# A shared ring for loads, checks and low halves, a sixth bonus by VectorE, and a new issue order

## The chip, the cores and the metric

One core of a Trainium2 chip runs the whole program. The metric is device time in microseconds (us) of one execution, lower is better; the number quoted for a kernel is the median of its runs.

## The reference

Two parts follow each other. The first is a recurrence over 768 steps for 4 batches and 8 heads of 48; the second is a gated MLP with a spatial product over the sequence.

```python
for t in range(S):
    kt, vt, rt, wt = (k[:, :, t], v[:, :, t], r[:, :, t], w[:, :, t])
    cur = np.einsum('bhd,bhe->bhde', u[None] * kt, vt)
    y[:, :, t] = np.einsum('bhd,bhde->bhe', rt, state + cur)
    state = wt[:, :, :, None] * state + np.einsum('bhd,bhe->bhde', kt, vt)
...
h = np.maximum(x @ w_in, 0.0)
u, v = (h[..., :d_ff // 2], h[..., d_ff // 2:])
...
v_n = (v - mu) / np.sqrt(var + 1e-06)
v_s = np.einsum('ts,bsd->btd', w_spatial, v_n) + b_spatial[None, :, None]
gated = u * v_s
return (gated @ w_out).astype(np.float32)
```

`x` is `y` with its heads laid side by side (384 columns), `d_ff` is 1024, all arrays are fp32. The part of `cur` with `u` adds, at each step and head, (sum over d of r·u·k) times v. It is called the bonus below.

## The kernel before, in words

**The recurrence in 24 slots.** The sequence is cut into chunks of 128 steps, so a batch has 6 and the program has 24 slots, i = 0 to 23. `slot_load` (L406 to L420) brings a slot's w (W, L415), k and r (kr, L416), in most slots r and k once more in natural order (N, 384 KB, L419), and v (L420). `slot_prep` (L433 to L537) prepares them: pairwise products of w (W2, L471), k and r scaled by w (L475), two scans F and E (L478, L483), the scaling of k and r by them (L485, L489). `slot_a` multiplies k by r within chunks of 64 on TensorE (PE, L552) and VectorE (DVE) puts the result under a mask into the matrix AS (L556); `slot_kt` transposes k (L571), `slot_y` and `slot_inter` multiply AS and the state by v and r (L588), and products L644 with L659, L670 and L672 carry the state on. `slot_x` collects `y` (L692, L699), transposes it (L704) and splits it into fp32r high and low halves `xT` (L715, L718, L723).

**The bonus, in two ways.** For i < B_PE = 6, `rk` = r·k (L443) goes through four fp32 products with u on PE (`pg`, L448), DVE multiplies v by the sums (`bv`, L518), and one fp32 product with the unit matrix adds `bv` to `y` in PSUM (L598). From slot 6 on the sums come from the natural order: N·N (L496), times u (L498), a sum over each head (L500), small copies (`dgs`, L524), which are put on the diagonal of AS (L532 on ScalarE, L534 on DVE or GpSimd); so the product with AS holds the bonus. At slot B_PE the part of PSUM that L598 began is cleared once (L602).

**The checks of w.** 16 loads Nw of 384 KB (L429) and one ScalarE instruction each (L430) see to it that w is in the range for which the fast way is right.

**The gMLP.** Products of three fp32r passes (`mm3`, L728 to L730: high·high, high·low, low·high): `ph` (v half of the hidden layer), `pu` (u half), `pv` (spatial product, on `vh` and `vl`, L804), `po` (output). `g_unit` adds the bias on DVE (L978), multiplies by u (L980), and splits into gh and gl (L983); `out_unit` copies `po` out (L997) and stores (L1006), the first SPLIT = 8 outputs in two halves of 64 rows. The last batch takes a different arrangement of the products, with s1, s4 and q2.

**What sets the order.** Every operation is recorded with the engines that could do it. The string PLAN holds one word for each: a letter for the engine and a rank in base 36. Operations are issued in the order of the rank, and each engine and each queue keeps that order: SP issues all loads and stores, one behind the other. ZEROS puts runs of zero products (L1084) at given points of PE's stream. They write to an unused part of PSUM.

**Buffers.** A `Buf` names a tag, and a tag a ring of so many places. When the order is known, `place` gives each buffer the place whose last reader comes first in the order. A load into a place then waits for that reader. N, Nw, `rk` and q2 have the tag "N" with one place; the low halves of `xT`, s1 and s4 and the raw loads of two of the weight groups share "xT1" with three places; gh and gl have five places each.

Of the kernel before, what the change touches and what calls it, by code (L numbers as in the profile page):

```python
# [9 lines left out]
F32R = mybir.dt.float32r  # L10
I32 = mybir.dt.int32
# [9 lines left out]
DM = H * D  # L21
# [85 lines left out]
"""  # L107

ZEROS = """
1:8 d:5 u:7 1a:7 1o:5 1y:6 2j:2 f8:1  # L110
"""

FILL_TO = 5

EARLY = 8

W3 = 5

KR, AB = 3, 2

SPLIT, PE_END = 8, 10

B_PE = 6

LOW_T, SUM_T = {}, 0

Q = 32
T = D - Q

class Buf:

# [107 lines left out]
def kernel(  # L241
# [15 lines left out]
    P = 128  # L257
# [148 lines left out]
    def slot_load(i):  # L406
# [4 lines left out]
        if i >= B_PE:  # L411
            N = q["N"] = buf(p2, [P, 2, DM], "N", f"N{i}", 1)
# [812 lines left out]
```

## Time and profile before

| | |
|---|---|
| time, median of 3 runs | 356.73 us (356.66 to 357.18) |
| profiled execution, its own time | 358.06 us |
| its span | 356.3 us |
| PE busy, products | 348.8 us (98%) |
| DVE busy | 282.0 us (79%) |
| ACT, POOL busy | 218.5 us (61%), 134.7 us (38%) |
| DMA | 50.17 MB, mean 141 GB/s |

PE is the matrix engine TensorE, PEld its weight loads, DVE is VectorE, ACT is ScalarE, POOL is GpSimd, SP issues the DMAs (SPq is its queue). Busy times are of one profiled execution; neighbouring products on PE overlap in the records, so the distance from start to start says what one costs in a row. A releaser, behind "<-", is what ended an engine's wait. L12 is line 12 of the kernel.

### The profile page before, as it was taken

The page shows a single profiled execution, that of the slowest core. Times are in us where ns is not written, and L with a number is a line of the kernel's source. Part 1 is how long each engine was busy: PE and PEld are TensorE (multiplying, and loading weights), DVE is VectorE, ACT ScalarE, POOL GpSimd, SP SyncE. Part 2 cuts the span into 40 slices and gives each one's busy share as a digit, 9 for nine tenths or more (in the row PEclk, how much of TensorE's full clock was granted, in tenths as well). Part 3 has the DMA queues.
Part 4 walks back from the last instruction along what each step waited for, and adds up shares of the span by engine and source line. Part 5 has one row for each costly group of instructions (what it writes and reads, how often), then busy time and mean ns, then how long its engine had stood idle before and what let it go on. Part 6 is the DMA issues. An engine that isn't in the chain of part 4 may idle for free.

```text
span 356.3 us, 11397 instructions
## 1 busy us (share of the span) xinstructions
PE 348.8 (98%) x4638; PEld 324.9 (91%) x4638; DVE 282.0 (79%) x634; ACT 218.5 (61%) x594; POOL 134.7 (38%) x188
## 2 busy tenths in 40 slices
PE   7999899999999999999999899999999999999998
PEld 7887798999999889899989799899998998899997
DVE  7999998989969798898965889467655679879771
ACT  5559977986556786886455764772427538574230
POOL 2364262115671632231172444335643810402540
PEclk9999999999999999999999999999999999999999
DMA  7867776634545667464464355264422344211013
GB/s 213 269 191 220 227 208 206 210 116 118 162 124 166 166 174 229 146 183 124 106 207 119 115 146 147 53 204 129 130 68 89 93 126 129 54 62 43 2 44 116
DMA packets 23736, 50.17 MB, mean 141 GB/s; under 512 B 3200, under 2 KB 12544, under 8 KB 23680
## 3 DMA queue, kind: packets, MB, share of 16 engines
q1 hardware_dynamic: 23536, 49.21, 46.8%
q8 instruction: 37, 0.61, 0.8%
q10 hardware_dynamic: 144, 0.20, 0.1%
q14 instruction: 19, 0.16, 0.1%
HBM read 44.67 MB, written 4.72 MB: 139 GB/s over the span
## 4 chain that ended last, share of the span: by engine, by line
PE 79%; DVE 7%; DMA 5%; issue 4%; ACT 2%; POOL 1%; SPq 0%; DVEq 0%; ACTq 0%; POOLq 0%
PE pv L730 6%; PE pv L728 6%; PE pv L729 6%; PE py L588 6%; PE po L728 4%; PE po L730 4%; PE po L729 4%; PE pu L728 4%; PE pu L730 4%; PE pu L729 4%; PE ph L728 4%; PE ph L730 4%; PE ph L729 4%; PE paw L552 3%; PE pt L571 2%
## 5 line engine op out<-in xcount | busy, mean ns | idle before, releaser
L728 PE MATMUL pv<-ws,vh 128*128 128x384 f32 x144 | 49.4, 343 | 0.0
L730 PE MATMUL pv<-ws,vl 128*128 128x384 f32 x144 | 48.9, 340 | 0.1
L729 PE MATMUL pv<-ws,vh 128*128 128x384 f32 x144 | 48.6, 338 | 0.0
L728 PE MATMUL po<-wo,gh 128*128 128x384 f32 x96 | 33.3, 346 | 1.4 <-DVE t L978 1.3
L728 PE MATMUL pu<-xT,wi 128*128 128x384 f32 x96 | 33.1, 345 | 0.0
L730 PE MATMUL pu<-xT,wi 128*128 128x384 f32 x96 | 32.4, 337 | 0.0
L729 PE MATMUL pu<-xT,wi 128*128 128x384 f32 x96 | 32.3, 336 | 0.0
L730 PE MATMUL po<-wo,gl 128*128 128x384 f32 x96 | 32.3, 336 | 0.0
L729 PE MATMUL po<-wo,gh 128*128 128x384 f32 x96 | 32.2, 336 | 0.0
L728 PE MATMUL ph<-wi,xT 128*128 128x512 f32 x72 | 29.2, 405 | 0.0
L730 PE MATMUL ph<-wi,xT 128*128 128x512 f32 x72 | 28.3, 393 | 0.0
L729 PE MATMUL ph<-wi,xT 128*128 128x512 f32 x72 | 28.2, 391 | 0.0
L730 PEld LDWEIGHTS pv<-ws,vl 128*128 128x128 f32 x144 | 27.0, 188 | 0.6 <-DVE vl L804 0.6
L728 PEld LDWEIGHTS pv<-ws,vh 128*128 128x128 f32 x144 | 27.1, 188 | 0.4 <-ACT vh L802 0.3
L729 PEld LDWEIGHTS pv<-ws,vh 128*128 128x128 f32 x144 | 27.1, 188 | 0.2
L475 POOL TENSOR_TENSOR kr<-kr,W 112x256 f32<-112x256 f32 x19 | 17.1, 904 | 25.3 <-DMA kr<-in_tr_dram 9.6
L758 ACT ACTIVATE hv<-ph 128x512 f32<-128x512 f32 x24 | 14.3, 596 | 16.7 <-PE ph L730 16.4
L532 ACT ACTIVATE AS<-id,dgs 128x64 f32<-128x64 f32 x68 | 18.1, 337 | 6.9 <-DVE dgs L524 5.6
L978 DVE TENSOR_TENSOR t<-pv,b_sb 128x384 f32<-128x384 f32 x24 | 13.2, 552 | 11.4 <-PE pv L730 10.2
L670 ACT ACTIVATE S<-S,prod 112x48 f32<-112x48 f32 x72 | 18.2, 323 | 5.7 <-DVE S L659 3.2
L728 PEld LDWEIGHTS po<-wo,gh 128*128 128x128 f32 x96 | 18.0, 188 | 2.7 <-DVE t L978 1.6
L430 ACT ACTIVATE Nw<-Nw,few 128x768 f32<-128x768 f32 x16 | 15.0, 938 | 7.8 <-DVE prod L480 2.5
(265 smaller groups left out, 1047.1 us busy)
## 6 DMA issues: line engine op xcount, KB each, us to landing
kr<-in_tr_dram SPq DMA_DIRECT2D x24, 448.0 KB, 4.9
N<-in_nat_dram SPq DMA_DIRECT2D x18, 384.0 KB, 3.3
Nw<-in_gt_dram SPq DMA_DIRECT2D x16, 384.0 KB, 3.4
W<-in_tr_dram SPq DMA_DIRECT2D x24, 225.8 KB, 4.0
v<-in_nat_dram SPq DMA_DIRECT2D x24, 192.0 KB, 3.9
out_dram<-ot SPq DMA_DIRECT2D x15, 192.0 KB, 2.0
wst<-in_w_spT_dram SPq DMA_DIRECT2D x12, 192.0 KB, 5.8
a<-in_w_spT_dram SPq DMA_DIRECT2D x12, 192.0 KB, 2.4
```

What stands on the lines that cost most here:

```text
L430: op({"A": 0.95}, lambda: nc.scalar.activation(flat(), flat(), AF.Relu, bias=neg, accum_out=over[:, n:n + 1]), r=[(w, 0)], w=[(w, 0), ("ov ...
L475: op({"G": 0.9, "V": dve(half)}, lambda e, n=n: e.tensor_tensor(two(kr()[:R, n])[:, :, :, n], two(kr()[:R, n])[:, :, :, n], w_()[:, :, :, ...
L532: e.mul(As()[:, j, g, :], id64, dgs()[:, j, g:g + 1])
L552: nc.tensor.matmul(pa()[ks, j, g * L:(g + 1) * L], kr()[rs, 0, ts_], kr()[rs, 1, ts_], start=True, stop=True)
L571: nc.tensor.transpose(pt()[:, g, :], kr()[:R, 0, g * C:(g + 1) * C], ident[:R, :R])
L588: nc.tensor.matmul(py()[row][L * a:L * (a + 1), D * n:D * (n + 1)], x, z, start=(a, row) not in started, stop=not left[0], skip_group_chec ...
L670: e.mul(S1[i % 2][a][:, g, :], S0[:, g, :], Wc[:, g:g + 1])
L728: nc.tensor.matmul(ps, ah, bh, start=first, stop=False, **skip)
L729: nc.tensor.matmul(ps, ah, bl, start=False, stop=False, **skip)
L730: nc.tensor.matmul(ps, al, bh, start=False, stop=last, **skip)
L758: op({"A": 0.61}, lambda: nc.scalar.activation(hv(), ph(), AF.Relu, accum_out=col(0)), r=[(ph, 0)], w=[(hv, 0), (s, 0, j)])
L978: op({"V": dve(HT)}, lambda: nc.vector.tensor_tensor(t1(), pv()[:, :HT], b_sb[:, tsl], ALU.add), r=[(pv, 0), ("b", 0)], w=[(t1, 0)])
```

## The change

The tag "N" goes. N, Nw, `rk` and q2 take places in the ring "xT1", which now has four. The ring of gl has four places instead of five. B_PE is 5: slot 5 takes the second way to the bonus, with a load of N more and no `rk`, `pg`, `bv`. SPLIT is 7: one output fewer is stored in two halves. PLAN and ZEROS are new; ZEROS holds 36 zero products for 41.

```diff
-1:8 d:5 u:7 1a:7 1o:5 1y:6 2j:2 f8:1
+b:9 h:4 n:2 12:8 1m:4 1y:6 3c:3
...
-SPLIT, PE_END = 8, 10
+SPLIT, PE_END = 7, 10
...
-B_PE = 6
+B_PE = 5
...
-        d = buf(pm, [P, KX * HT], raw, f"d_{key}", 3, I32)
+        d = buf(pm, [P, KX * HT], raw, f"d_{key}", 3 + (raw == "xT1"), I32)
...
-            N = q["N"] = buf(p2, [P, 2, DM], "N", f"N{i}", 1)
+            N = q["N"] = buf(pm, [P, 2, DM], "xT1", f"N{i}", 4)
...
-        w = buf(p2, [P, 2, DM], "N", f"Nw{n}", 1)
+        w = buf(pm, [P, 2, DM], "xT1", f"Nw{n}", 4)
...
-            rkt = buf(p2, [P, 2, DM], "N", f"rk{i}", 1)
+            rkt = buf(pm, [P, 2, DM], "xT1", f"rk{i}", 4)
...
-            xT[b, h] = tuple(buf(pm, [P, KX, HT], f"xT{q}", f"xT{b}_{h}_{q}", 3, F32R) for q in range(2))
+            xT[b, h] = tuple(buf(pm, [P, KX, HT], f"xT{q}", f"xT{b}_{h}_{q}", 3+q, F32R) for q in range(2))
...
-        q2 = buf(p2, [P, 2, DM], "N", "q2", 1)
+        q2 = buf(pm, [P, 2, DM], "xT1", "q2", 4)
...
-        gh, gl = gg[b, h, f] = tuple(buf(pm, [P, HT], n, f"{n}{b}_{h}_{f}", 5, F32R) for n in ("gh", "gl"))
+        gh, gl = gg[b, h, f] = tuple(buf(pm, [P, HT], n, f"{n}{b}_{h}_{f}", 5 - (n == "gl"), F32R) for n in ("gh", "gl"))
```

The new order moves operations on every engine. Three places follow, as names of tiles with their numbers (a slot's, or batch, half and part).

**PE, at the products of slot 5 with v.** Before, from the transposes of slot 4's `y`:

```order
L704 MATMUL yt4_1014<-ident_94,y4_949 128x128 x3
L718 MATMUL yt3_978<-xT0_1_0_1022,nident_110 128x384
L598 MATMUL py0_88<-bv5_974,ident_94 128x384
L718 MATMUL yt4_1014<-xT0_1_0_1022,nident_110 128x384
L588 MATMUL py0_88<-v5_875,AS1_86 64x48
L588 MATMUL py1_89<-v5_875,AS1_86 64x48
```

and now:

```order
L571 MATMUL pt6_1071<-ident_94,kr6_979 128x112 x4
L718 MATMUL yt4_1023<-xT0_1_0_859,nident_110 128x384
L588 MATMUL py0_88<-v5_967,AS1_86 64x48
L588 MATMUL py1_89<-v5_967,AS1_86 64x48
L588 MATMUL py1_89<-vs5_984,AS1_86 64x48
```

The product with `bv5` (L598) and, further ahead, the four of `pg5` are gone; the first product of slot 5 begins on the cleared PSUM.

**SP, the loads from N17 to v17.** Before:

```order
L419 DMA N17_3161<-in_nat_dram 128x768
L416 DMA kr17_3168<-in_tr_dram 112x1024
L420 DMA v16_3226<-in_nat_dram 128x384
L415 DMA W18_3320<-in_tr_dram 112x516
L429 DMA Nw9_3325<-in_gt_dram 128x768
L420 DMA v17_3330<-in_nat_dram 128x384
L419 DMA N18_3365<-in_nat_dram 128x768
```

and now:

```order
L420 DMA v16_3104<-in_nat_dram 128x384
L419 DMA N17_3106<-in_nat_dram 128x768
L416 DMA kr17_3129<-in_tr_dram 112x1024
L419 DMA N18_3205<-in_nat_dram 128x768
L429 DMA Nw10_3226<-in_gt_dram 128x768
L415 DMA W18_3301<-in_tr_dram 112x516
L420 DMA v17_3364<-in_nat_dram 128x384
```

N18 stood behind the check Nw9 and behind v17, and now stands right behind kr17, ahead of both.

**DVE, ahead of the sum for `y8`.** Before:

```order
L983 TENSOR_TENSOR gl0_1_0_1903<-t10_1_0_1549,gh0_1_0_1896 128x384
L475 TENSOR_TENSOR kr10_1893<-kr10_1893,W10_1801 112x256 x2
L482 RECIPROCAL zz_80<-prod_133 112x8
L659 TENSOR_TENSOR S0_116<-paw_87,S110_119 112x192
L997 COPY ot0_0_1_1999<-po0_0_1_1822 128x384
L483 SCALAR_TENSOR_TENSOR E10_2011<-W2p_83,zz_80 112x256
L715 CAST xT1_0_0_1797<-yt7_1995 128x3x128
L556 COPY_PREDICATED AS1_86<-mask_130,paw_87 128x512
L659 TENSOR_TENSOR S0_116<-paw_87,S111_120 112x192
L699 TENSOR_TENSOR y8_2014<-y8_2014,py1_89 128x384
```

and now:

```order
L997 COPY ot0_0_2_1981<-po0_0_2_1804 128x384
L983 TENSOR_TENSOR gl0_1_0_1984<-t10_1_0_1686,gh0_1_0_1915 128x384
L534 TENSOR_TENSOR AS0_85<-id64_107,dgs10_1789 128x256
L471 TENSOR_TENSOR W2p_83<-W11_1923 112x256
L556 COPY_PREDICATED AS1_86<-mask_130,paw_87 128x512
L534 TENSOR_TENSOR AS0_85<-id64_107,dgs10_1789 128x256
L659 TENSOR_TENSOR S0_116<-paw_87,S110_119 112x192
L692 COPY y8_2038<-py0_88 128x384
L496 TENSOR_TENSOR N12_1844<-N12_1844 128x384
L478 SCALAR_TENSOR_TENSOR F11_2041<-zz_80,W2p_83 112x256
L500 TENSOR_REDUCE dg11_2043<-N11_1770 128x8
L699 TENSOR_TENSOR y8_2038<-y8_2038,py1_89 128x384
```

Ahead of `y8` now also stand a third output copy, L471 and L478 for slot 11, N12's product and the sum `dg11`, and y8's first copy (L692), which ACT did before; the scan for `E10` and its reciprocal have gone further ahead, the copy into `xT1_0_0` to ScalarE. `gl0_1_0` has moved behind `ot0_0_2`.

## Rows read from the trace of the kernel before

**Rows 1.** The page: busy time, share and count of each engine; DVE's slices.

```profile
PE 348.8 (98%) x4638; PEld 324.9 (91%) x4638; DVE 282.0 (79%) x634; ACT 218.5 (61%) x594; POOL 134.7 (38%) x188
...
DVE  7999998989969798898965889467655679879771
```

**Rows 2.** Table by stages: stretch, length, busy us (count) of PE, PEld, DVE, ACT, POOL, clock, DMA.

```profile
0.00:72.00 72.00, 67.55 (x1114) 59.64 (x1115) 65.92 (x148) 53.05 (x139) 25.61 (x43) 1.00 0.73 216
72.00:125.00 53.00, 52.64 (x720) 49.76 (x719) 44.52 (x100) 36.00 (x110) 25.51 (x32) 1.00 0.51 144
...
195.00:207.00 12.00, 10.74 (x163) 10.10 (x162) 9.92 (x24) 8.58 (x25) 4.64 (x6) 1.00 0.42 121
```

**Rows 3.** Chain of waits, 188 to 205 us: start, us, what.

```profile
193.16 5.32 DMA N<-in_nat_dram
...
199.09 1.15 DVE dgs L524
...
202.38 0.47 DVE t L978
...
202.90 0.44 PE po L728
```

**Rows 4.** PE's waits (releaser, total us, times, longest); DVE's timeline at 198 us.

```profile
PE paw L552 <- issue: 1.3, 1, 1.3
PE po L728 <- DVE t L978: 1.3, 1, 1.3
...
198.50 0.56 DVE L496 TENSOR_TENSOR N<-N 128x384 f32<-128x384 f32 x1 [1.30 <-DMA N<-in_nat_dram]
```

**Rows 5.** SP's waits: whole span, then 185 to 203 us; the page's DMA issues of N.

```profile
SPq L419 <- ACT Nw L430: 23.9, 7, 5.1
...
SPq L420 <- PE py L588: 5.3, 1, 5.3
...
N<-in_nat_dram SPq DMA_DIRECT2D x18, 384.0 KB, 3.3
```

**Rows 6.** Timeline of PE at slot 5's bonus: start, us, instruction.

```profile
44.54 1.05 PE L448 MATMUL pg<-up_sb,rk 112*128 112x2 f32 x8
45.45 0.42 PE L728 MATMUL pu<-xT,wi 128*128 128x384 f32 x1
...
56.13 0.81 PE L598 MATMUL py<-bv,ident 128*128 128x384 f32 x2
56.68 0.44 PE L718 MATMUL yt<-xT,nident 128*128 128x384 f32 x1
```

**Rows 7.** Zero products in the chain of waits at 17 us.

```profile
17.19 1.31 PE py L1084 x10
```

**Rows 8.** DVE by form: line, shapes, xcount, busy us, mean ns, idle before.

```profile
L475 DVE TENSOR_TENSOR kr<-kr,W 112x256 f32<-112x256 f32 x29 | 13.5, 469 | 0.0
L489 DVE TENSOR_TENSOR kr<-kr,E 112x512 f32<-112x512 f32 x16 | 11.4, 710 | 0.2
...
L496 DVE TENSOR_TENSOR N<-N 128x384 f32<-128x384 f32 x14 | 8.0, 573 | 1.5 <-DMA N<-in_nat_dram 1.5
...
L498 DVE TENSOR_TENSOR N<-N,u_sb 128x384 f32<-128x384 f32 x13 | 7.2, 551 | 0.1
...
L518 DVE TENSOR_TENSOR bv<-v,pg 128x384 f32<-128x384 f32 x6 | 3.3, 542 | 0.0
...
L443 DVE TENSOR_TENSOR rk<-kr 112x512 f32<-112x512 f32 x4 | 2.8, 690 | 0.2 <-DMA kr<-in_tr_dram 0.2
```

**Rows 9.** POOL's N·u by form; POOL and DVE side by side (timelines).

```profile
L498 POOL TENSOR_TENSOR N<-N,u_sb 128x384 f32<-128x384 f32 x5 | 5.4, 1089 | 13.7 <-DVE N L496 13.2 <-ACT y L692 0.5
...
123.95 1.06 POOL L485 TENSOR_TENSOR kr<-kr,F 112x496 f32<-112x496 f32 x1
...
124.59 0.83 DVE L496 TENSOR_TENSOR N<-N 128x384 f32<-128x384 f32 x1
...
198.82 1.40 POOL L804 TENSOR_TENSOR vl<-hv,vh 128x512 fp32r<-128x512 f32 x1 [1.56 <-ACT vh L802]
```

More of the change, by code (lines that the diff above doesn't have):

```diff
@@ new lines @@
+Aaa Aab S54 S4z S5y S7v V6k V6j V67 V6y V75 V78 V7h V72 G7o G6i V6p V6s A8r A81 V80 A7c A7q G8l A8n T87 V8w G8j T7i
+A7n V8z T9b T7w V8v V99 T9g A9j V9k T9m A9s Ta3 Aa6 Taf Tag Tak Aar Aas Aat Aau Vb8 Vbd Vbf Vbg Gbk Vbn Vbs Abx Aby
+Vc5 Ac1 Acb Vcc Ack Acp Vcr Tnz T5m T63 T65 A66 Tc6 Tcd Tcf Tcu Td7 Td8 Vdu Ved Aem Vey T69 T6h T6l A71 Tc7 Tcn Tco
+Tcz Td0 Tdd Vdo Gfw Ag8 Vg9 T6x T70 T7j A8b Tdc Tdl Tdm Tdn Tdt Tdz Veq Ves Agd Vgm T7r T7s T8d A8u Tc2 Tce Tcw Tcx
+Td4 Td5 Vd6 Vdr Af2 Ggb Tgu Tgw Tgy Tgz Vh6 Shx Thj Thl Thm Ti0 Vi3 Skc Thc The Ti2 Tim Vj3 Slo Tac Taq Tb5 Aba Tfa
@@ new lines @@
+V118 G11h V121 V172 G15x V13m A127 A14x A13n G14y T15a V15y G166 T124 V125 T173 T159 V167 G16a V16c T174 A17g V17h
+T17r A17s V17t T183 T184 T18a A191 A192 A194 A19c V19l V19t V1a5 V1a6 G1aa G1ae G1af A1am V1b0 A1b4 V1br V1ag V1av
+A1cq G1d0 A1ba V1bg A1ci V1d9 S18p A1a2 S12q S154 S10e S15t G142 V158 V16s V143 V144 V15h V15n G15i G16x G136 G137
+V147 V16o A165 V148 V150 A16e G18k G16i T16y V18o A16r T15j V15p T190 T16z V178 G17b V186 T195 A1ak V1ao T1b1 V1be
+V1bf T1c1 T1c2 T1c4 A1cr A1cs A1df S14q A14r S13o S170 S12j S189 G162 G17u V176 V16g V177 V18j V18n G185 V1a8 G12t
@@ L107 @@
+T1gv T1h6 V1hb T1gk T1h3 T1h4 V1ha T1gq T1gy T1h0 V1hs V1i1 A1i8 V1i9 T1gt T1hc T1hf V1hh V1hx A1i6 G1ih T1hk T1hl
+T1hm V1ho V1ir A1is V1iz T1hg T1hr T1hv V1i2 V1iw A1j1 V1j2 T1ht T1hw T1i3 V1id G1ie A1if G1il T1i4 T1i5 T1i7 V1ij
+G1im A1in V1iv T1i0 T1ia T1ib T1ii A1ik S1ji T1hn T1ic T1ip T1iq V1j3 S1j5 T1he T1ig T1io T1it A1iu S1j4 T1jd T1je
+T1jf T1jk A1jl S1jo T1ix T1iy T1j6 T1j9 V1jg S1jh T1j7 T1j8 T1ja T1jb V1jc S1jj V1j0 T1jm V1jn
 """
 ZEROS = """
-1:8 d:5 u:7 1a:7 1o:5 1y:6 2j:2 f8:1
+b:9 h:4 n:2 12:8 1m:4 1y:6 3c:3
@@ L833, in g_unit_last @@
     def g_unit_last(b):
-        s1, s4 = (tuple(buf(pm, [P, KX, HT], f"xT{p}", f"s{n}_{p}", 3, F32R) for p in range(2)) for n in (1, 4))
+        s1, s4 = (tuple(buf(pm, [P, KX, HT], f"xT{p}", f"s{n}_{p}", 3+p, F32R) for p in range(2)) for n in (1, 4))
         either = {"V": dve(HT), "G": pool(HT)}
@@ L960, in g_unit @@
         t1 = buf(pm, [P, HT], "w3", f"t1{b}_{h}_{f}", W3)
-        gh, gl = gg[b, h, f] = tuple(buf(pm, [P, HT], n, f"{n}{b}_{h}_{f}", 5, F32R) for n in ("gh", "gl"))
+        gh, gl = gg[b, h, f] = tuple(buf(pm, [P, HT], n, f"{n}{b}_{h}_{f}", 5 - (n == "gl"), F32R) for n in ("gh", "gl"))
         for k_ in range(KX):
@@ L1065, in general @@
                                       .rearrange("o (k p) s -> p (o k) s", p=P))
-                    hi, lo = xT["g", h] = tuple(buf(pm, [P, KX, HT], f"xT{q}", f"gxT{h}_{q}", 3, F32R) for q in range(2))
+                    hi, lo = xT["g", h] = tuple(buf(pm, [P, KX, HT], f"xT{q}", f"gxT{h}_{q}", 3+q, F32R) for q in range(2))
                     nc.scalar.copy(hi(), xf)
```

136 lines of the change are left out of this document (61 added, 75 removed).

## The prediction

> **What bounds the kernel now.** I read the page first, then a table by stages, then the waits of the stages in which TensorE stopped. The page shows TensorE (PE) busy 98% of the span, VectorE (DVE) 79%; in the slices DVE is at 9 in nearly all of the first ten and lower behind [rows 1]. The table by stages [rows 2] says it in numbers, at the full granted clock throughout. From 0 to 72 us DVE is busy 65.9 of 72 us: here the two engines feed each other, and PE, busy 67.6, still stops for DVE, which sets the pace. From 72 to 125 us PE lacks 0.4 us, while DVE has 8.5 us of 53 idle. Behind that PE stops for long in one place only, from 195 to 207, where it lacks 1.3 us of 12. So the time is the moment at which DVE lets PE through the first stage, plus the PE work that is left, plus that stop.
>
> The stop has a cause in a transfer. PE waits for `t` of L978 once, 1.3 us [rows 4]. The chain of waits [rows 3] goes from SP's issue of N at 193.16 over a landing of 5.32 us to L496, L524 and L978 on DVE and to the first `po` product at 202.90; DVE sat 1.30 us for that N [rows 4]. SP had issued it late: ahead of it in SP's queue stood `v`, whose place a PE group held for 5.3 us, and a check of w; N and the checks take turns in one place, and over the program SP waits 23.9 us in 7 times at L419 for a check to leave it [rows 5].
>
> **The change, part by part.**
>
> *The sixth bonus.* PE loses four fp32 `pg` products (8 records) and one `bv` product (2 records). In PE's stream the eight stand from 44.54 to the next product at 45.45, 0.91 us, and the two from 56.13 to 56.68, 0.55 [rows 6]. Together 1.5; their busy times, 1.05 + 0.81 = 1.9, overlap with neighbours and are the upper end. It is no gain by itself: it lies in the stage that DVE paces, and counts only through the PE work left behind it.
>
> *Zero products.* Five passes fewer, two records each. The longest run of them in the chain of waits is ten records in 1.31 us [rows 7], so five passes are 1.3 us of PE work. They fill time in which PE would wait for DVE, so I cost them at nothing; if PE were the limit there, −1.3.
>
> *DVE in the first stage.* On DVE, slot 5 loses `rk` (0.69) and `bv` (0.54) and gains N·u (0.55) [rows 8], the sum over a head and a copy; its N·N goes to POOL. That is about even. But the table also moves other work. I added up DVE's queue in both orders, each instruction at the usual duration of its form. Up to `y5`, the sixth chunk's `y`, four of L489 (4 × 0.71 = 2.8) have gone behind it or to POOL, and some eight others; ahead of it have come three of L475 (0.47 each) and ten others [rows 8]. The sum falls by 1.0. Up to `vl0_5`, the low half that PE's first spatial products take just as DVE has it, it falls by 1.5. The PE work behind that product, counted record by record at the trace's spacing, rises by 0.3. **First stage: −1.5 + 0.3 = −1.2.** Bounds: 0 if the room is lost to waits that move along, −2.8 (1.5 + 1.3) if PE alone were the limit.
>
> *DVE from 80 to 120 us.* This is the other side of the same table. Up to `y8` DVE's sum grows by 4.6 (among others four more L475 and three more L496, against three fewer L489); from `vl0_5` to `y8` that is 4.6 + 1.5 = 6.1 us more. PE has 1.8 us more to do in the same stretch, which covers 1.8. So DVE must find 4.3 us in idle time, of which 72 to 125 us hold 8.5 [rows 2]. Up to `y15` the excess has turned into −1.0. The price lies between 0 (all found) and 4.3 (the idle time consists of waits that move along). I take **+1.3**, a third: there is twice as much idle time as needed, but part of it is waits for PE and ACT in the wrong place. What is queued behind the added work is `gl0_1_0`, now behind `ot0_0_2`, and the two steps of `y8`, the first of which DVE takes over from ACT; `po` and the transposes of `y8` on PE wait for them.
>
> *The ring for N.* N, the checks of w and `rk` may now stand in any of four places, shared with the activations' low halves. N18, the load of the stop at 201 us, stood behind a check of w and behind v17; it stands now ahead of both, next to kr17. DVE's wait of 1.30 goes if SP gets there some 2 us sooner. What is late next in that chain is the copy of L524 and L978 itself [rows 3], which wait for nothing else there. I take **−1.3**; ends 0 and −1.4. The other waits at L419 cost nothing now, since PE shows no stop for them. Of N there are now 19 loads for 18, 384 KB and 3.3 us each [rows 5]: the new one is issued among the first, long before slot 5's sum is due, which covers it; without that cover it would be 3.3 once.
>
> *The `gl` ring of four, the stores.* A fifth `gl` can no longer be written before the last `po` of the half has read the first; only `gl0_1_0` shows this in the order, and that is in the term for 80 to 120. One output fewer is stored in halves: an SP issue fewer, 0, since SP has no deadline there. PE's stop of 1.3 us at L552 with no releaser [rows 4] lies in the stage that DVE paces: 0, ends −1.3 and +1.3.
>
> *POOL.* Of the products on N, 19 for 9 are POOL's, at 1.09 us each against 0.55 on DVE [rows 8, 9]. POOL is busy 38%. What it costs depends on what stands beside it: while POOL was at L485 from 123.95 for 1.06 us, DVE's L496 took 0.83 instead of 0.57; and in the chain at 199 the small copy of L524 took 1.15 and ended with POOL's L804, which began at 198.82 and took 1.40 [rows 3, 9]. So a meeting can cost from 0.3 to 1.0 us. I cost it at 0, since DVE has idle time where the ten stand; ends 0 and +2.0, two full meetings in a chain that PE waits for. The Trainium skill, SBUF — State Buffer, section "Who interferes with whom", has it that VectorE and GpSimd share one pair of ports as an exclusive lock: a VectorE instruction with two SBUF inputs blocks until a GpSimd instruction that reads SBUF is done. By that rule each of the ten would cost DVE up to its whole length, and it speaks against this move; the two rows agree with it.
>
> **The sum.** −1.2 + 1.3 − 1.3 = −1.2. Against the profiled execution, 358.06 us (span 356.3 and 1.8 around it), that is 356.9. That execution lies 1.3 over the median of the runs shown, 356.73, so for the median I say **355.5 us**. About 0.2%, 0.7 us, is what a measurement of this kernel can tell from no change: faster is below 356.0, slower above 357.4.
>
> **Rivals.**
> - *PE is the limit all through.* DVE's idle time takes the added work, and the bonus and the zeros count in full: −2.8 − 1.3 = −4.1, 352.6. For: PE at 98%, and twice the idle time that DVE needs. Against: before 72 us PE still lacks 4.4 us.
> - *DVE becomes the limit from 80 to 125 us (the other side).* The 4.3 is paid in full: −1.2 + 4.3 − 1.3 = +1.8, 358.5. It decides once over 3.2 of the 4.3 is not found in idle time. For: DVE is busy 84% there, and its idle time is waits. Against: PE has products there that need nothing new of DVE.
> - *The ring does not bring N forward.* With three low halves alive one of the four places is free; SP then waits for that one instead, and every load behind it too: −1.2 + 1.3 = +0.1, 356.8. For: SP waits often at L419 already [rows 5]. Against: a check holds its place only for its landing and one ACT instruction.
> - *POOL's products hold DVE up in a chain to PE.* Two full meetings of 1.0 us in a chain like that at 199: −1.2 + 2.0 = +0.8, 357.5. For: [rows 9]. Against: DVE is idle 16% of 72 to 125 us. The page of the Trainium skill named above has the rule by which it would come.
>
> **How the numbers follow.** Forecast 0.41 (its own range 354.2 to 356.0), PE-bound 0.13, idle ring 0.18, DVE-bound 0.19, POOL's meetings 0.09. Faster 0.41 + 0.13 = 0.54, same 0.18, slower 0.19 + 0.09 = 0.28. To hold the time 8 times in 10 the range reaches from the PE-bound case, 352.6, to just under the DVE-bound one, 358.4.
>
> **What would show it.** Right: `y5` and the product on `vl0_5` come 1 to 1.5 us sooner; DVE doesn't wait for the transfer of N near 200, and `po` doesn't stop there; DVE is near 95% from 80 to 125 us, and PE lacks under 2 us there. The DVE-bound case would show as PE waits of 3 us or more in all on `AS` (L556), `gl` or `y` between 80 and 150. The idle ring would show as SP waits at L419 on `xT`, with N18 as late as before; the meetings as DVE copies of 0.9 us and more beside POOL's N. The forecast is wrong if the stage before 80 us gets no shorter.

## The result, and the profile after

The changed kernel takes **361.28 us** (median of five executions, 358.01 to 362.66) against 356.66 for the kernel before (355.49 to 357.18): a ratio of 1.011, interval [1.008, 1.0139]. It is slower by about 1.1%, and over the top of the predicted range, 358.4. The profiled execution is the fastest of the five, 358.01 us with a span of 356.3; that of the kernel before took 358.06 with the same span. So **the two profiles show a draw**, and the loss lies in what executions do that the profiled one does less of. One column of the list of executions points at it: the mean granted clock of TensorE was 0.995 in three and 0.991 in two of the five, the profiled one among the three; the kernel before had 1.000 in 21 of the 23 executions that were measured beside the first experiments. The column isn't the whole of it: at the same 0.995 the three executions stand at 358.01, 359.98 and 361.28. Medians here and below are of all executions; ratios and intervals leave out those that took over 1.5% more than the fastest of the same kernel.

The page of the changed kernel, for [rows 1] (busy, then the granted clock in 40 slices):

```profile
PE 347.8 (98%) x4618; PEld 323.3 (91%) x4618; DVE 286.6 (80%) x642; ACT 222.0 (62%) x598; POOL 142.4 (40%) x185
...
PEclk9998999999999999999999999999999999999999
```

The table by stages, for [rows 2] (stretch, length, busy of PE, PEld, DVE, ACT, POOL, clock, DMA):

```profile
0.00:72.00 72.00, 67.53 (x1103) 59.37 (x1104) 65.61 (x156) 55.94 (x150) 27.48 (x44) 0.98 0.77 221
72.00:125.00 53.00, 50.62 (x709) 48.17 (x708) 51.41 (x107) 34.82 (x103) 18.89 (x19) 1.00 0.53 158
...
195.00:207.00 12.00, 12.00 (x213) 11.64 (x203) 9.53 (x26) 6.92 (x17) 4.71 (x11) 1.00 0.55 162
```

Three things differ. The clock is 0.98 in the first stage. From 72 to 125 us DVE is busy 51.4 of 53 us (44.5 before), and PE now lacks 2.4 us there (0.4 before). From 195 to 207 PE lacks nothing (1.3 before). PE's waits, for [rows 4], say which stops these are (total us, times, longest):

```profile
PE yt L704 <- DVE t L978: 1.7, 1, 1.7
PE py L588 <- issue: 1.4, 1, 1.4
PE paw L552 <- DVE S L659: 0.7, 2, 0.5
PE pv L728 <- DVE t L978: 0.5, 1, 0.5
```

The stop of `po` near 201 is gone. SP issues N18 at 184.21 instead of 193.16 [rows 3], and its waits at L419 for a check's place have shrunk from 23.9 us [rows 5] to 3.7:

```profile
184.21 0.33 SPq L419 DMA_DIRECT2D N<-in_nat_dram  x1
187.11 0.33 SPq L429 DMA_DIRECT2D Nw<-in_gt_dram  x1
```

The new stop stands at 100.7 us. Timelines of DVE and POOL ahead of it (start, us, instruction; the last row is PE's):

```profile
97.23 1.02 POOL L498 TENSOR_TENSOR N<-N,u_sb 128x384 f32<-128x384 f32 x1
...
97.86 1.77 DVE L983 TENSOR_TENSOR gl<-t,gh 128x384 fp32r<-128x384 f32 x1
...
98.20 1.02 POOL L983 TENSOR_TENSOR gl<-t,gh 128x384 fp32r<-128x384 f32 x1
...
100.08 0.54 DVE L978 TENSOR_TENSOR t<-pv,b_sb 128x384 f32<-128x384 f32 x1
...
100.68 0.55 PE L704 MATMUL yt<-ident,y 128*128 128x128 f32 x3 [1.67 <-DVE t L978]
```

DVE's `gl` takes 1.77 us where the next one, at 100.88, takes 0.55, and it ends 0.4 after POOL's second product in a row: the meeting that the prediction bounded at 0.3 to 1.0 costs DVE 1.2 here. The Trainium skill, SBUF — State Buffer, "Who interferes with whom", has a VectorE instruction with two SBUF inputs wait until a GpSimd instruction that reads SBUF is done; the rows agree, here for two in a row.

The other stop is one "with no releaser". Before, one of this kind ended at 44.04, just ahead of slot 5's `pg` [rows 6]; now one ends at 24.5, and behind it the granted clock falls. PE's timeline, first of the kernel before, then of the changed one, and windows of the changed one around the stop (stretch, length, busy of the engines, granted clock, DMA):

```profile
44.04 0.57 PE L552 MATMUL paw<-kr 48*64 48x64 f32 x21 [1.34 <-issue]
...
22.93 0.22 PE L588 MATMUL py<-v,AS 64*64 64x48 f32 x2
24.52 0.26 PE L588 MATMUL py<-vs,AS 64*64 64x48 f32 x2 [1.37 <-issue]
```

```profile
22.00:23.00 1.00, 1.00 (x62) 0.98 (x62) 0.50 (x1) 0.70 (x2) 0.00 (x0) 1.00 0.96 295
23.00:24.50 1.50, 0.15 (x9) 0.04 (x3) 1.36 (x3) 1.50 (x6) 0.00 (x0) 1.00 0.63 180
24.50:26.00 1.50, 1.48 (x70) 1.42 (x70) 1.10 (x2) 1.02 (x3) 0.00 (x0) 1.00 0.95 303
26.00:26.50 0.50, 0.50 (x7) 0.50 (x6) 0.50 (x3) 0.27 (x1) 0.00 (x0) 0.93 0.77 247
26.50:29.50 3.00, 3.00 (x15) 3.00 (x16) 3.00 (x8) 1.29 (x3) 2.52 (x2) 0.50 0.84 237
```

PE had worked without a long gap, stood still for 1.4 us, worked again for 2 us at the upper level (2.4 GHz), and then had 1.2 GHz for 3.4 us; "PE busy 3.00 of 3.00" is a busy engine at half pace (15 products). The busy share doesn't show this, the clock column does.

The profiles, term by term. The work behind the product is a count of PE's records by kind: both kernels have the same number of each kind there, but for two zero products fewer in the changed one (0.13 us each). The others come from the timelines and from the table by stages.

| term | predicted | profile against profile |
|---|---|---|
| PE's first product on `vl0_5` | −1.5 | 71.95 → 70.47: −1.5 |
| PE work behind that product | +0.3 | −0.3 |
| DVE, 72 to 125 us (PE's lack) | +1.3 | 0.36 → 2.38: +2.0 |
| PE's lack from 195 to 207 us (N18) | −1.3 | 1.26 → 0: −1.3 |
| rest | 0 | +1.05 |
| sum | −1.2 | −0.05 |

Of the rest, 0.3 us is PE's lack from 125 to 195 us (0.04 before, 0.35 now); most of the remainder is that the same products follow each other at wider spacings, which no run here explains.

### The profile page after: what moved, and what is told of

It is laid out like the page before. It is cut to its first block, busy times and chain, and to the rows that moved or that the text cites. A ratio compares the mean times of both kernels' runs of the same rounds, so it can differ in the third digit from the quotient of the medians.

```text
span 356.3 us, 11363 instructions
## 1 busy us (share of the span) xinstructions
PE 347.8 (98%) x4618; PEld 323.3 (91%) x4618; DVE 286.6 (80%) x642; ACT 222.0 (62%) x598; POOL 142.4 (40%) x185
## 4 chain that ended last, share of the span: by engine, by line
PE 68%; DVE 3%; issue 1%; ACT 0%; POOL 0%; POOLq 0%; DVEq 0%
PE pv L728 5%; PE pv L730 5%; PE pv L729 5%; PE po L728 4%; PE po L730 4%; PE po L729 4%; PE py L588 4%; PE ph L728 3%; PE ph L730 3%; PE ph L729 3%; PE pu L730 3%; PE pu L728 3%; PE pu L729 3%; PE paw L552 2%; PE paw L644 2%; PE yt L704 2%
## 5 line engine op out<-in xcount | busy, mean ns | idle before, releaser
L730 PE MATMUL pv<-ws,vl 128*128 128x384 f32 x144 | 48.6, 338 | 0.0
L730 PE MATMUL pu<-xT,wi 128*128 128x384 f32 x96 | 32.5, 338 | 0.0
L730 PE MATMUL po<-wo,gl 128*128 128x384 f32 x96 | 32.3, 336 | 0.0
L730 PE MATMUL ph<-wi,xT 128*128 128x512 f32 x72 | 28.3, 393 | 0.0
L730 PEld LDWEIGHTS pv<-ws,vl 128*128 128x128 f32 x144 | 27.0, 188 | 0.0
L485 POOL TENSOR_TENSOR kr<-kr,F 112x496 f32<-112x496 f32 x14 | 15.1, 1079 | 27.1 <-DVE kr L475 15.2
L670 ACT ACTIVATE S<-S,prod 112x48 f32<-112x48 f32 x84 | 21.2, 325 | 3.2 <-DVE S L657 2.1
L556 DVE COPY_PREDICATED AS<-mask,paw 128x512 f32<-128x512 int32 x24 | 17.7, 738 | 3.8 <-PE paw L552 2.4
L659 DVE TENSOR_TENSOR S<-paw,S 112x192 f32<-112x192 f32 x40 | 13.9, 348 | 6.2 <-ACT S L670 2.6
L478 DVE TENSOR_TENSOR_SCAN F<-zz,W2p 112x256 f32<-112x256 f32 x24 | 16.4, 684 | 2.8 <-POOL W2p L471 2.5
```

The source lines that it names most:

```text
L478: op({"V": 0.69}, lambda: nc.vector.tensor_tensor_scan(flat(F())[:, ::-1], zF[:, ::-1], W2()[:, :0:-1], 0.0, ALU.max, ALU.mult), r=[(W2, 0 ...
L485: op({"V": 0.68, "G": 1.07}, lambda e: e.tensor_tensor(seg(kr()[:R, 0])[:, :, :L2 - 1], seg(kr()[:R, 0])[:, :, :L2 - 1], F()[:, :, 1:].uns ...
L556: op({"V": 0.735}, lambda: nc.vector.copy_predicated(As(), mask.unsqueeze(1).unsqueeze(1).broadcast_to([P, 2, G, L]), pa()[:, :, :G * L].r ...
L659: nc.vector.tensor_tensor(S0, pd(), S1[i % 2][a], ALU.add)
L670: e.mul(S1[i % 2][a][:, g, :], S0[:, g, :], Wc[:, g:g + 1])
L730: nc.tensor.matmul(ps, al, bh, start=False, stop=last, **skip)
```

## The experiments

Below, the kernel before is measured anew on the chip of each job (356.7 to 357.2 us), and ratios are against it. "Clock" is the mean granted clock of one execution. A pass in ZEROS is two zero products, 0.26 us of PE; the 36 and 41 given with the change are passes. Where operations were moved by number, two lines were added ahead of L207, so the lines of that profile stand two higher.

### Zero products put back: e1, e5, e9, e12

```diff
-b:9 h:4 n:2 12:8 1m:4 1y:6 3c:3
+b:9 h:4 n:2 12:8 1m:4 1w:4 1y:6 3c:3
```

This is e1: four passes at 17 us, where PE had stood 0.47 us. They don't close that gap: in the profiles PE waits 0.7 us ahead of them, for ScalarE's copy of `y` (L692).

> The changed kernel with one run of four zero products more, in the gap of 0.45 us that PE has at 16.9 us waiting for DVE, ahead of the masked products of slot 1. Theory clock: the changed kernel loses because PE's granted clock falls to half at 26.5 us for 3.3 us, after a stop of 1.37 us at 22.9 and gaps at 16.9 and 20.9. If the gap at 16.9 had its part in the fall, the clock stays at 1.000 and the median is 2 us or more below the changed kernel's 361.3. If the stop alone brings the fall, clock and time stay as they were (0.995 or 0.991, 360 to 362). Theory DVE (the changed kernel loses only between 72 and 125 us, to DVE and POOL): time unchanged within 1 us, whatever the clock does.

358.45 us (356.99 to 364.47), ratio 1.0032 [1.0007, 1.0057]. It adds 1.0 us of PE work, and the time falls by 2.8; the interval lies under the changed kernel's. The clock was 1.000 in 9 of 12 executions, with a median of 357.4. One of the other three was profiled, 363.01 us. There the clock falls behind the second stop, and the execution also has the slow start that the last section tells of:

```profile
101.00:103.50 2.50, 0.82 (x53) 0.70 (x46) 2.50 (x5) 1.43 (x4) 0.96 (x1) 1.00 0.31 36
103.50:107.00 3.50, 3.50 (x14) 3.50 (x15) 2.71 (x7) 2.76 (x8) 0.82 (x1) 0.55 0.66 218
```

e5 adds six passes by that stop (`go:6`), and e9 five more in the first place (`b:14`).

> The changed kernel with the four zero products at 16.9 us of the run e1_zeros_gap and six more (1.3 us) in the stop of 1.67 us that PE has at 100.7 us, ahead of the transposes of slot 6. Nothing real is moved. Theory clock, now with two places: in e1_zeros_gap the clock was at 1.000 in 9 of 12 executions (median of these 357.4), and where it fell it fell at 103.5, behind this stop. Then the clock is at 1.000 in nearly all executions, and the median is 357 to 357.6, against 358.5 there and 361.3 for the changed kernel. Rival (the falls come from the stops themselves, or from elsewhere): 3 in 12 or more executions still show a clock below 1.000, and the median stays above 358.

> The changed kernel with zero products at three places: the first run from 2.3 us back to 14 as in the kernel before (9 in the changed one), four at 16.9 us and six ahead of the transposes of slot 6, as in e5_zeros_both. Theory start: in two profiled executions of 363 us PE worked at half speed (a pass of zeros in 0.22 instead of 0.11 us a record) until 11.8 and 12.5 us, in all others until 6.3 or 6.4; the changed kernel's first zeros end at 6.3, just there, those of before at 7.6. With 14 the late rise is gone: no execution of 12 over 359, median 357 or under (358.0 in e5_zeros_both, with 3 of 12 over 359.5). Rival (the spread has another cause, loads that come late or DVE): the tail over 359.5 stays and the median stays at 358.

e5: 358.01 (356.99 to 360.8; 357 to 357.6 was expected), 1.0041 [1.0016, 1.0065], clock 1.000 in 11 of 12. e9: 358.9 (357.64 to 361.02), 1.0038 [1.0007, 1.0069], 1.000 in all 12. So with these passes the clock is held, and the time comes down by 2.4 to 3.3 of the 4.6 us; more zero products give no more. These runs alone don't tell how: the stop at 24.5 us, 1.37 in the changed kernel, is 0.7 in e1's profile and absent in e5's and e9's, so the clock may have stayed up because the stop went (e17 and e18 below bear on this). The expectation that e9 has no executions over 359 failed (five of 12). In e9's profile PE's stop at 100.7 has turned into zero products (the first row is the last eight of twelve) and PE is busy 52.16 of the 53 us:

```profile
99.25 1.06 PE L1084 MATMUL py<-zk 128*128 128x128 f32 x8
100.44 0.55 PE L704 MATMUL yt<-ident,y 128*128 128x128 f32 x3
```

but y6's transposes come 39.84 us behind y5's, as in the changed kernel (60.60 to 100.44, and 60.84 to 100.68): the passes hold the clock, and don't shorten the time that DVE takes.

e12 has the five passes in the first place alone.

> The changed kernel with the first run of zero products alone back to 14, no other edit. Theory start and fall are two things: the late rise goes, the fall at 26.5 and that at 103 stay (clock 0.995 or 0.991 in most executions), and the median comes down from 361.3 by 1 to 2 us, to 359.3 to 360.3. If the start has no part: 361 as before. If the shift of 20 instructions also moves PE's stop for its own instructions at 22.9 us, the fall at 26.5 goes too, and the median is 358 or less.

360.13 (357.28 to 361.84), 1.0062 [1.0025, 1.0099]. Within one kernel the time goes with the clock: 357.3 to 357.8 in the three executions at 1.000, 359.7 to 360.2 in the four at 0.995, 360.2 to 361.8 in the five at 0.99.

### Zero products taken out: e4, e10, e13 (kernel before), e15, e16 (changed kernel)

e4 drops `1o:5` of the kernel before, e10 drops `d:5`, e13 all but the first two places:

```diff
-1:8 d:5 u:7 1a:7 1o:5 1y:6 2j:2 f8:1
+1:8 d:5
```

> The kernel before, with five zero products fewer: the run of ten records that stood at 17.1 us is left out, nothing else. The prediction priced five fewer at nothing, since they fill time in which PE waits for DVE: then the time stays within 0.3 us of before. Theory clock: the granted clock falls below 1.000 in some or all executions and the time rises by 1 us or more.

> The kernel before with the first run of zero products cut from 14 to 9, nothing else; the mate of e4_before_few_zeros, which left five out at 17 us and stayed level (356.4 against 356.8). Theory start: some executions (3 in 12 or more) rise to 359 to 361 and the median by 0.5 to 3 us. Rival (zeros cost nothing wherever they stand, as the prediction priced them): level with before within 0.5 us, no tail.

> The kernel before, with the zero products taken out everywhere but in the first two places (28 passes of two products, 7.3 us of PE work at 0.13 us each). Clock theory: the stops that they filled are left open, PE's granted clock falls behind some of them in nearly every execution, mean clock 0.97 to 0.995, and the time is 358 to 363 us although 7.3 us of PE work are gone; the profile shows two or more stretches at 0.50. Prediction's step (zero products fill time that PE waits anyway and cost nothing): 356 to 357 at clock 1.000. PE-bound rival: 349.5 to 353 at clock 1.000.

e4: 356.41, 0.9981 [0.9958, 1.0003], clock 1.000 in 10 of 12. e10: 358.43, 1.0023 [0.999, 1.0055], below 1.000 in 9 of 12. e13: 356.36, **0.9995 [0.996, 1.0029]**, with a clock of 0.981 in eight executions and 0.967 to 0.971 in four. The eight took 354.8 to 357.2 us, the four 359.1 to 361.3. So e13 is as the clock theory says in the clock, and in the median as the prediction says in the time. Its windows show why both can be:

```profile
12.50:26.00 13.50, 11.88 (x167) 10.38 (x170) 11.94 (x27) 6.63 (x19) 4.84 (x7) 0.50 0.69 191
26.00:72.00 46.00, 45.91 (x800) 39.24 (x793) 44.16 (x100) 40.20 (x108) 16.11 (x19) 1.00 0.71 210
```

PE has 1.2 GHz for 13.5 us, yet `y5`'s transposes start at 61.32 (61.34 in the kernel before). Behind the slow stretch PE lacks 0.1 us up to 72 (the stop at 44 us is gone), and it has 7.3 us of zero products less to do in the whole program: slower products fill the time that DVE leaves.

The same edit in the changed kernel (e15: `b:9 h:4` alone; e16 with `go:6` besides):

> The changed kernel, with its zero products taken out everywhere but in the first two places (23 passes, 46 products, 6.0 us of PE work at 0.13 us each). Place theory, formed after e13 (a fall of the granted clock costs time only where PE sets the pace; before y5, at 61 us, VectorE does): a long stretch at 0.50 between 10 and 30 us, y5's transposes still at 60 to 61.5, no stop for PE's own instructions at 24; the stop at 101 with the fall behind it stays and costs 1.5; mean clock 0.97 to 0.98, median 357 to 359, so 2 to 4 under the changed kernel as given although the clock is lower. Rival (the changed kernel needs its zero products for the clock, and more would be better): y5 after 62.5, falls in three or more places, median 361 to 364.

> As e15, with six passes at the place of e5's second addition, by the stop at 101 us. Place theory: as e15 up to there, no fall behind the stop at 101, y8's transposes at 121 to 122, median 356 to 357.5. Rival: the falls ahead of 61 us decide, and it stands within 1 us of e15, both over 360.

e15: 362.03 (360.09 to 363.94), 1.0139 [1.0098, 1.0181]. e16: 364.38, 1.0185 [1.014, 1.023]. My place theory fell. Of the rival the median of e15 came; its three falls didn't (the profile shows one, with `y5` at 62.44), and e16 isn't within 1 us of e15 but 2.4 above. In e15 the half-speed stretch is as long as in e13, but behind it PE lacks 1.6 us, for 0.1 in e13:

```profile
13.00:26.50 13.50, 11.98 (x194) 10.20 (x189) 11.53 (x26) 7.73 (x23) 4.22 (x6) 0.51 0.64 184
26.50:72.00 45.50, 43.91 (x754) 37.64 (x749) 41.94 (x101) 40.67 (x111) 17.44 (x19) 1.00 0.75 218
```

`y5`'s transposes start at 62.44, for 60.84 in the changed kernel. So the kernel before can do without its zero products at the same median. The changed one doesn't gain by losing them, as the place theory had it, and no loss is shown either: e15's interval overlaps the changed kernel's own, [1.008, 1.0139]. It is e1, e5 and e9, with passes added, that stand under both. That the changed kernel's first stage has less room since DVE's part of it is 1.5 us shorter fits, but is argued. e16 fills the stop at 101, and a stop "issue" of 1.8 at 182 takes over with a fall of its own.

### What makes the two stops: e2, e3, e6, e14, e17, e18

e2 issues the load of one weight group (`wu2`) later, so that less data is under way at 16 to 24 us.

```diff
+        for n, (on, start) in {74: ('S', 98.5), 75: ('A', 137.5)}.items():
+            self.ops[n].on, self.ops[n].start = on, start
```

> The changed kernel with one load of 512 KB (a weight block that is used only from 33 us on) issued at about 23.7 instead of 17.4 us, and its first conversion put behind it. Theory fetch: PE's stop at 22.9 to 24.5, which has no releaser, comes from a 16 KB fetch of its own instructions that stood behind data in the DMA engines (it began at 21.9, 5.3 us after PE had entered the block before; in other places 1 to 2 us). With a fifth less data in the queue the fetch begins 1.5 us or more sooner, the stop goes, the granted clock stays at 1.000, and the median is 2 to 4 us below the changed kernel's 361.3. Rival: the stop belongs to the order of PE's small products and not to DMA; then stop, clock and time stay.

361.59, 1.0148 [1.0097, 1.0198]. The stop was 0.8 us instead of 1.4. That doesn't show that the data held the fetch up, since the stop is 0.7 to 1.8 us in variants whose loads are issued as in the changed kernel (e1, e3, e12, e17, e18). The falls stayed, at 26.5 and at 102 us (clock 0.986 to 0.995), and so did the time:

```profile
26.50:30.00 3.50, 2.94 (x14) 2.60 (x14) 3.20 (x7) 2.05 (x7) 2.50 (x2) 0.56 0.87 279
...
102.00:105.50 3.50, 3.50 (x12) 3.50 (x13) 2.79 (x7) 2.52 (x7) 0.74 (x1) 0.51 0.66 213
```

The second has a price: from `y5`'s to `y8`'s transposes it is 62.7 us here (62.8 in e1 and in e3, which fall there too), and 61.2 in the changed kernel's profile, in e9 and in e12, which don't: **1.5 us**. A long fall at 26 (6.8 us, e12) puts `y5`'s transposes at 63.6, 3.0 behind e9; since e9's profile lacks the stop too (1.8 us in e12), this is the price of stop and fall together. The kernel before shows a fall by itself: e4's profile has the stop at 44 us as before (1.39 us, 1.34 before), then 6.8 us at 1.2 GHz, and `y5`'s transposes come **2.9 us** later (64.23, 61.34 before). The short fall in the changed kernel's own profile isn't seen in `y5` (60.8; 60.6 in e9).

e3 gives slot 10's N·u to DVE (`760: ('V', 580)`), e6 exchanges it with POOL's `gl` (`760: ('G', 587.5), 761: ('V', 605.5)`, and `1w:4`).

> The changed kernel with one product, N times u of slot 10, on DVE instead of POOL, at the same place in the order. In the trace of the changed kernel a split on DVE took 1.77 us instead of 0.57 beside POOL's N times u at 97.2, and PE stopped 1.67 us at 100.7. Theory meeting (POOL holds DVE up): that split takes 0.6 to 0.9 us, PE's stop falls by about 1 us, and the median falls by up to 1 us. Theory load (DVE has too much to do from 80 to 125 us): the 0.55 us more on DVE make the stop longer by about half a microsecond.

> The changed kernel with the four zero products at 16.9 us, and with two instructions moved in the order: N times u of slot 10 stands behind a split on POOL instead of ahead of it, and the sum over it on DVE behind the addition that frees PE's PSUM place. The stop at 100.7 us came from a split on DVE that took 1.77 us beside POOL's N times u and the next split. Theory meeting: the DVE split takes 1.0 us or less, the addition comes about 1.1 us sooner, PE's stop there falls to 0.6 us or less, the clock stays, and the median is 356 to 356.8, level with before. Theory load (DVE simply has too much to do from 80 to 125 us): the wait shows up at the next product that needs DVE, PE loses 2 us or more from 72 to 125 us all the same, and the median stays at 358.

e3: 361.65, 1.0106 [1.007, 1.0141]; the stop becomes a wait of `py` for `AS`, 1.4 us. DVE's `gl` is back at 0.54, but DVE's N·u now takes 1.61 beside POOL's `t` and `gl`: the meeting has moved along. e6: 358.48, 1.0058 [1.0023, 1.0092]. It didn't take the meeting apart: DVE's `gl` still has two POOL products beside it and takes 1.78, and the stop is 1.3.

e17 and e18 take it out of that place: that `gl` goes to POOL, and N·u and its sum behind the `t` for which PE waits; e17 also has `1w:4`.

```diff
+        for n, (on, start) in {423: ('G', 585), 760: ('G', 606), 761: ('V', 608)}.items():
+            self.ops[n].on, self.ops[n].start = on, start
```

> e1 (four zero passes put back at 17 us), and the meeting at 97.9 us taken apart: the split gl of half 0, part 1 goes from VectorE to POOL, and POOL's product N times u of slot 10, and the sum behind it, behind the t of half 1 for which TensorE's stop at 101 us waits. Meeting theory (VectorE's gl took 1.77 instead of 0.55 because POOL had two products in a row beside it; e6 had only exchanged those two): the stop before y6's transposes goes from 1.7 to under 0.3, nothing falls at 103, the stretch from y5's to y8's transposes is 60 us or less instead of 61.2, and the median is 356 to 357.5. Load theory (VectorE is full from 72 to 125 us, so the work only moves): a stop of 1 us and more appears at another place before y8, the stretch stays at 61 to 61.5, median 358 to 359.

> The same meeting taken apart, with the changed kernel's own zero products. Meeting theory: the stop at 101 goes, the fall behind it too, the one at 26 us stays; clock 0.995 in most executions, median 358 to 360 for 361.3. Load theory: as the changed kernel, 361 to 362, falls behind another stop in 72 to 125 us.

e17: 360.0 (356.5 to 364.32), 1.0041 [1.0001, 1.0082]. e18: 359.39 (357.19 to 361.9), 1.0058 [1.0029, 1.0087]. The stop at 101 shrinks to 0.5, and another takes its place; PE's waits in e18:

```profile
PE pt L573 <- POOL kr L487: 1.4, 1, 1.4
PE py L590 <- issue: 1.1, 1, 1.1
...
PE yt L706 <- DVE t L980: 0.5, 1, 0.5
```

It ends at 104.8, behind the products that POOL now does later, and the clock falls behind it from 105 to 108.5. A stop of over 1 us in another place is what the load theory expected; its medians (358 to 359 for e17, 361 to 362 for e18) didn't come. The meeting hasn't gone but moved: in e18 DVE's scaling of k and r at 100.38 (L489 of the kernel) takes 1.50 us beside POOL's N·u, where it takes 0.68 in e6 and e14. So no run here has this stretch without a meeting, and whether the load or the meetings make the stop stays open.

e18 and e17 differ by the four passes at 17 us alone, and both have the stop of PE with no releaser at 24 to 25.5 us, of 1.1 and 1.2. Behind it the clock falls in e18's profile and not in e17's (a stretch some 3 us behind the stop, first in e18, then in e17 with its stop; stretch, length, busy of the engines, granted clock, DMA):

```profile
27.00:27.50 0.50, 0.50 (x4) 0.50 (x4) 0.50 (x4) 0.22 (x1) 0.50 (x2) 0.50 0.72 156
...
PE py L590 <- issue: 1.2, 1, 1.2
28.50:29.00 0.50, 0.50 (x7) 0.50 (x7) 0.50 (x3) 0.02 (x1) 0.50 (x2) 1.00 1.28 307
```

So with the same stop the passes go with a held clock, in one profile of each; the clock was 1.000 in 6 executions of 12 in e18 and in 9 in e17. In time they bring nothing in this order: 359.39 without them, 360.0 with them.

e14 takes four copies, 1.9 us, from DVE to ScalarE between 92 and 119 us, with e5's zero products.

> The changed kernel with the zero products of e5 (two more places), and four of VectorE's copies between 92 and 119 us (two output copies, y8's first copy, one copy of v) given to ScalarE, 1.9 us of VectorE. Load theory (VectorE paces 72 to 125 us, and what is left over the kernel before at clock 1.000 is lost there): PE's busy time in 72 to 125 us rises from 52.1 towards 53, y8's transposes come 0.5 to 1.5 us sooner than at 121.9, and the median falls from 358.0 to 356.5 to 357.5. Rival (with zero products put back PE is already full there, and what is left is the PE work of the zero products): PE busy and y8 within 0.3 us of e5, median 357.8 to 358.5. Second rival: ScalarE, which also puts AS's diagonal and the transposes' copies on their way, becomes late: PE waits for ACT of 1 us and more in that stretch, and a median over 358.5.

358.76, 1.0086 [1.0058, 1.0114]. PE is busy 52.38 us there for 52.13 in e5, and from `y5`'s to `y8`'s transposes it is 61.2 in both: as the rival has it, relieving DVE brings PE nothing there with the zero products in place. The rival's median, 357.8 to 358.5, was missed by 0.3.

e8, e6 with three more passes at 101 us (`go:3`), held the clock at 1.000 in all ten executions and took 359.05, 1.0081 [1.0052, 1.011]; a wait for `v` of 0.9 us was new.

> Both together: the zero products at 16.9 us, the two moves of e6_no_meeting, and three zero products ahead of the transposes of slot 6. If the clock and the meeting are all that the changed kernel loses by, the clock is at 1.000 in nearly all executions and the median is 355.5 to 356.5, under before. If DVE's load is behind it, 357.5 or more.

### The bonus alone: e7, e11

In the kernel before, B_PE = 5, with slot 5's products on N given to DVE (e7) or to POOL (e11), the small copies to ScalarE or DVE, and the load of N put among slot 5's loads; ring and table else as before.

```diff
-B_PE = 6
+B_PE = 5
```

> The kernel before with the sixth bonus alone taken from PE: slot 5 gets a load of N, N times N, N times u and the sum on DVE in the places of its old product and near them, the copies on ACT, the diagonals on ACT and POOL, the clearing of PSUM a slot sooner; no ring, no other order. Theory of the prediction: PE's 1.5 us less of work lie in the stage that DVE paces, and DVE gets about 0.8 us more there, so the gain is small: 0 to 0.8 us under before. Rival (PE is the limit): 1.3 to 1.6 us under before. Rival clock: PE is left with gaps where the products stood, the clock falls in some executions, and the median rises by 1 us or more.

> The kernel before with the sixth bonus alone taken from PE, as e7_bonus_alone, but with the two products on N and both diagonals on POOL and the small copies on DVE; there ACT, which had them, held PE up for 2.7 us at 55.8 and the clock fell behind it. DVE now has about 0.2 us more in the stage, PE 1.5 us less. Theory of the prediction: DVE paces that stage, so 0 to 0.8 us under before. Rival (PE is the limit): 1.3 to 1.6 us under. Rival clock: a stop comes where the products were, the clock falls in half of the executions or more, and the median lies 2 us or more over before.

e7: 363.11, 1.0167 [1.0139, 1.0194]; e11: 362.51, 1.0102 [1.0049, 1.0154]. Both are slower, by stops that my placing made (PE waited 2.7 us for ScalarE's copy of `xT` in e7, 2.1 for DVE ahead of slot 5's products in e11), with a fall of the clock behind each (58 to 64.9 us and 52.3 to 55.7). So the first stage's saving without the new table isn't shown by itself.

## Why the prediction was wrong, and where it was right

- **Zero products: the step that failed.** "They fill time in which PE would wait for DVE, so I cost them at nothing." That holds for the kernel before (e13). In the changed kernel it doesn't: with four passes put back at one place PE's granted clock is 1.000 in 9 of 12 executions, for none of five, and the median is 2.8 us lower (e1); e5 and e9 hold the clock in 23 of 24 and are 3.3 and 2.4 lower. The prediction looked at a clock of 1.00 in every stretch [rows 2] and had no rival in which it falls. What falls cost where a profile shows them, 1.5 us behind the stop at 101 and 2.9 behind that at 44 (e4), is the size of what lies between the executions of 358 and of 362.7 us. That the clock is the way by which the passes bring the time is argued from these sizes: no execution of the changed kernel over 358.01 was profiled, and where e17 adds the same passes to e18's order, the time stays.
- **The median from one profile.** I subtracted from the profiled execution's time and carried the 1.3 us over to the median. The changed kernel's profiled execution lies 3.3 under its median, the other's 1.4 over; a draw in the profiles was a loss of 4.6 in the medians.
- **DVE from 80 to 120 us: right mechanism, too small.** PE lost 2.0 us, not 1.3, at the place that the prediction named (`t` and `gl` ahead of `y6` to `y8`). DVE is 97% busy, so "a third" of the excess was too kind. The rival with DVE as the bound said 358.5 by waits there; with the clock held the kernel is at 358.0 to 358.9, but it gets there in another way, with PE work (zero products) in the place of PE's waits (e9, e14).
- **POOL's meetings at 0.** One meeting cost DVE 1.2 us in the chain to PE (the rows at 97.86). What it is worth in time isn't settled: taken out of its place, the meeting and the stop moved on (e3, e17, e18). Of the prediction's two rows for a meeting, the small copy of L524 has a single input and doesn't bear on instructions with two.
- **PE's stop with no releaser at 0.** The stop itself is as long as before, 1.4 us. At 44 us it was harmless in most executions; at 24.5, behind a gap of 0.47 at 17, the clock falls behind it. In e4, where it fell behind the one at 44, the execution took 360.48.
- **First stage: right in its main part.** The first product on `vl0_5` comes 1.5 us sooner, `y5`'s transposes only 0.5 (1 to 1.5 was said). The +0.3 was wrong: no PE work has moved behind that product, which has two zero products fewer behind it (−0.3).
- **N18: right.** It is issued 9 us sooner, and PE doesn't stop near 201. SP's waits at L419 fell. The idle ring didn't happen for N18; later than 200 us one load of N waits 6.1 us for `pu` (L730), which reads `xT`, and PE has no stop over 0.5 us behind it.
- **The bonus's 1.5 us of PE work** and five passes (1.3): these 20 records are gone and all others are as before, 2.8 us by their spacing, as expected; since the span is the same, PE's stops and stretched spacings grew by as much.

Open: with the clock at 1.000 in all executions e8 and e9 still stand 0.4 to 0.8% over the kernel before, and their executions scatter from 357.6 to 362 us (from 355 to 359.2 in the kernel before at that clock). The slow start told of below explains some of them at most. Of the 2.5 to 3.4 us between the forecast and the versions that hold the clock, 0.7 is the term of DVE; the others aren't told apart. No version of the changed kernel came out under the kernel before.

## What to carry to other kernels

An engine whose clock depends on its being busy makes filler work part of the schedule: before it is costed at nothing, look for the longest stop that it leaves on that engine and ask what a fall of the clock behind that stop would cost. What such a fall costs depends on the place: 13.7 us at half pace were free in one profile (e13, which also had less filler to do), and 6.8 us cost 2.9 in another (e4). A profile is one execution: compare the granted clock of all executions before the sum of terms is carried over to the median.

## What the runs showed of the hardware

- **A clock that falls in a busy stream.** PE was busy 96 to 98% of the span in every kernel here, and yet single stops of 0.8 (e2) to 2.7 us (e7) were followed, at once or up to 3 us later, by 3.4 or 6.8 us at 1.2 GHz, and stops of 1.5 us left without zero products by 13.7 us (e13). Stops of the same length also passed without a fall: 1.34 us at 44 before, 1.67 at 101 in the changed kernel, 1.22 in e17. What decides between the two isn't shown.
- **PE waits for its own instructions.** The two stops "issue", at 44.04 before and at 24.52 after, come at PE's instructions number 1473 and 705 in the trace (products and weight loads counted), a distance of three times 256; in e1, e2, e3, e12, e17 and e18 it is number 705 too. A packet of 16 KB in the queue for instructions ended 1.35 us ahead of each (at 42.67 and 23.17). It had begun 4.5 and 5.3 us after PE passed the previous such edge, and at most 3.0 us after it at the other edges ahead of 60 us. In the changed kernel the DMA engines were busy 0.93 of the time from 17 to 23 us; that this made the packet late isn't shown (e2). The Trainium skill, Runtime: NRT & Kernel Launch, "Instruction fetch mechanics", has blocks of 16 KiB and 256 instructions, and calls the cost of crossing into one mostly hidden; the trace agrees on the block and shows 1.4 us not hidden.
- **A slow start that the clock column doesn't show.** In the changed kernel's profile eight `pg` products at 6.32 took 1.02 us together, in e1's, e3's and e16's 1.75 to 1.81, and products kept that pace until about 12 us, while the granted clock is given as 1.00. In e1 and e3 `y0`'s transposes came at 24.6, for 20.9 to 22.6 in the other variants of the changed kernel whose clock hadn't fallen by then, and `y5`'s at 63.6 and 63.1, for 60.6 to 60.8 in e5, e9 and the changed kernel: as dear as a fall. Rows of e1:

```profile
2.34 4.21 PE L1084 MATMUL py<-zk 128*128 128x128 f32 x18 [2.34 <-DVE py L303]
6.34 1.75 PE L448 MATMUL pg<-up_sb,rk 112*128 112x2 f32 x8
7.95 2.05 PE L1084 MATMUL py<-zk 128*128 128x128 f32 x8
```
